# A fused attention, gate and expert kernel: a fifth tile for the rounded queries and keys, and transfers and loads asked for earlier

## The chip, the cores and the metric

The kernel runs on one core of one Trainium2 chip. The metric is the device time of one execution in microseconds, and of several executions the median is taken. PE is the TensorE matmul stream, DVE VectorE, ACT ScalarE, POOL GpSimd, and SP the engine whose queue issues nearly all the transfers here.

## What is computed

Three steps run one after the other on the same data: a causal attention with a decay, a gated layer, and a routing of each token to one of eight experts with a capacity.

```python
cum = np.cumsum(np.log(np.clip(f, 0.0001, 1.0)), axis=-1)          # 4 x 8 heads, 576 tokens, 64 wide
scores = q @ k.T / 8 + cum[:, None] - cum[None, :]                 # -1e9 above the diagonal
attn = softmax(scores)                                             # sum + 1e-9
x = (attn @ v).transpose(0, 2, 1, 3).reshape(2304, 512)
x = (sigmoid(x @ w_gate) * (x @ w_val)) @ w_out                    # 512 -> 1536 -> 512
logits = x @ w_route                                               # top scores first, at most 288 tokens each
out[tokens of e] = np.maximum(x[tokens of e] @ w1[e], 0) @ w2[e]   # 512 -> 1024 -> 512
```

## The kernel before

Attention takes the first 195 us, the gated layer the stretch to about 620 us, and routing and experts the rest. The change lies in attention and in the work that is fitted between its heads for the layer behind it.

**One head.** Queries and keys of a head (64 x 576 each) are used as a rounded part and a remainder. ACT writes the rounded parts into one of four tiles `P1` (`prep`, L116: two copies). Rows 64 and 65 of that tile take the decay of the head, two rows of `ck`, by a transfer (`decay`, L122). A second tile `P2` takes the rounded parts again, by two transfers (`copies`, L125), and the remainders, by two subtractions on POOL (`query_low` L134, `key_low` L137). `maxparts` (L148) then does four matmuls into two banks `a` and `c` of the ring `p1b`, and two more into `pb`, from `P1` alone; after each group DVE takes a row maximum over it (`top`, L156), five per head into five columns of `mx`. What a `top` writes beside the maximum goes to `junk`, a tile that nobody reads; the five have ranges of their own in it. `mrows` (L180) transposes `mx` with one matmul, ACT copies it to `mr`, and `mstore` (L186) sends it into row 66 of `P1`. With these rows `scores` (L189) gives, in twelve matmuls, exponents that are below zero already; ACT takes their exponentials, POOL blanks what lies above the diagonal (L211), and `av` (L216) multiplies with the values.

**The order.** It is written out by hand. In the steady part of the loop (L300) a turn does `scores(h)`, and then `av(h-1)` with two pieces put between its matmuls: `early` (row 66 of head h+2, `prep(h+4)` and `decay(h+4)`) and `late` (`maxpass(h+3)`). The four `P1` tiles go round by `h % 4`, so `decay(h+4)` can run when `scores(h)` is done with its tile, and its rows are read by `maxpass(h+4)` one turn later. The first heads (L261 to L347) are written out one by one, with empty matmuls (`warm`) between them to keep PE going.

**Work between the heads.** `fill(h)` (L1210) assembles the first fifteen of 36 pieces of the layer's weights: a transfer to `mr0` or `mr1`, three bit operations on DVE into `mb0` or `mb1` (L435 to L441), a rounding on ACT (L449), a subtraction on POOL (L452). From head 15 it also gets 512 tokens of attention's output ready in four parts of four turns: turn 0 issues four transfers (`XLoader.load`: the output, and the reciprocal sums spread over 64 partitions), turn 1 multiplies the two on DVE (L496), turn 2 rounds on ACT, turn 3 subtracts on POOL.

Of the kernel before, what the change touches and what calls it, by code (L numbers as in the profile page):

```python
# [58 lines left out]
KT = [(0, 0, 0, 1024), (0, 128, 128, 0), (0, 256, 256, 512), (0, 384, 384, 832), (0, 448, 512, 448)]  # L59


def attention(ev, qk, vr, f, xs, rec, fill):

# [1 line left out]
    with ExitStack() as ctx:  # L67
# [2 lines left out]
        ps2 = ctx.enter_context(tc.tile_pool(name="att_p2", bufs=1, space=PSUM))  # L70
        ps1 = ctx.enter_context(tc.tile_pool(name="att_p1", bufs=2, space=PSUM))

        ft = st.tile([NHEAD, S], F32, name="ft")
        nc.sync.dma_start(ft, f)

# [18 lines left out]
        nc.gpsimd.memset(zero, 0.0)  # L94
        nc.scalar.activation(idle, zero, AF.Ln, bias=1.0)
        next(consts)
        P1 = [st.tile([67, 64 + 2 * S], F32R, name=f"P1_{i}") for i in range(4)]
        for t in P1:
            nc.gpsimd.memset(t[64:67].bitcast(F32), 1.0)
            nc.gpsimd.memset(t[0:64, 0:64].bitcast(F32), 0.0)  # L100

        junk = st.tile([128, 1600], BF16, name="mj")
        JT = (0, 64, 256, 576, 1024)
        ck = st.tile([NHEAD, 2, S], F32R, name="ck")
        next(consts)
        nc.vector.tensor_scalar(ft, ft, 1e-4, 1.0, op0=OP.max, op1=OP.min)
# [7 lines left out]
        Q0, K0 = 64, 64 + S  # L114

        def prep(h):  # L116
            p1, r = P1[h % 4], RAW[h]
            nc.scalar.activation(p1[0:64, Q0:K0], r[0:64], AF.Copy)
            nc.scalar.activation(p1[0:64, K0:], r[64:128], AF.Copy)
            P2[h] = wk.tile([128, 2 * S], F32R, name="p2", bufs=4)  # L120

        def decay(h):  # L122
            nc.sync.dma_start(P1[h % 4][64:66, K0:].bitcast(F32), ck[h:h + 1].bitcast(F32))

        def copies(h, keys=True):  # L125
            p1, p2 = P1[h % 4], P2[h]
            nc.sync.dma_start(p2[0:64, :S].bitcast(F32), p1[0:64, Q0:K0].bitcast(F32))
            if keys:
                nc.sync.dma_start(p2[64:128, S:].bitcast(F32), p1[0:64, K0:].bitcast(F32))

        def key_copy(h):
            nc.vector.tensor_copy(P2[h][64:128, S:], P1[h % 4][0:64, K0:])

        def query_low(h):  # L134
            nc.gpsimd.tensor_tensor(P2[h][64:128, :S], RAW[h][0:64], P1[h % 4][0:64, Q0:K0], op=OP.subtract)

        def key_low(h):  # L137
            r, p2 = RAW.pop(h), P2[h]
# [9 lines left out]
        def maxparts(h):  # L148


            p1 = P1[h % 4]
            q = lambda s, e: p1[0:66, Q0 + s:Q0 + e]
            k = lambda s, e: p1[0:66, K0 + s:K0 + e]
            mx = MR[h] = wk.tile([128, 5], F32R, name="mx", bufs=3)

            def top(t, src):  # L156
                n = src.shape[-1]
                nc.vector.tensor_tensor_reduce(out=junk[:, JT[t]:JT[t] + n], in0=src, in1=ev.mq[:, S - n:], op0=OP.add,  # L158
                                               op1=OP.min, scale=-1.0, scalar=3e38, accum_out=mx[:, t:t + 1])

            a = ps1.tile([128, 512], F32, name="p1b")
            c = ps1.tile([128, 512], F32, name="p1b")
            mm(a[:, 0:192], q(64, 192), k(0, 192), True, False)
            mm(a[:, 192:512], q(192, 320), k(0, 320), False, True)
            mm(c[:, 0:448], q(320, 448), k(0, 448), True, False)
            mm(c[:, 448:512], q(-64, 64), k(0, 64), False, True)
            for t, src in ((1, a[:, 0:192]), (2, a[:, 192:512]), (3, c[:, 0:448]), (0, c[:, 448:512])):
                top(t, src)
            yield
            b = MT[h] = ps2.tile([128, 1024], F32, name="pb")  # L170
            mm(b[:, 256:512], q(448, 576), k(0, 256), True, True)
            mm(b[:, 512:832], q(448, 576), k(256, 576), True, True)
            top(4, b[:, 256:832])
            yield
# [9 lines left out]
            nc.scalar.activation(MR[h], b[0:5, 0:128], AF.Copy)  # L184

        def mstore(h):  # L186
            nc.sync.dma_start(P1[h % 4][66:67, 0:640].bitcast(F32), MR.pop(h))

        def scores(h, m=None):  # L189
            p1, p2 = P1[h % 4], P2.pop(h)  # L190
            y = ps2.tile([128, 1024], F32, name="py")
            x = ps1.tile([128, 512], F32, name="p1b")
            z = ps1.tile([128, 512], F32, name="p1b")

            def sc(out, k0, q0, q1, first=True, last=True):
                mm(out, p1[0:67, K0 + k0:K0 + k0 + 128], p1[0:67, Q0 + q0:Q0 + q1], first, False)
                mm(out, p2[:, S + k0:S + k0 + 128], p2[:, q0:q1], False, last)

            sc(y[:, 256:512], 0, 0, 256)
            sc(y[:, 512:832], 0, 256, 576)  # L200
            sc(x[:, 0:448], 128, 128, 576, last=False)
            sc(x[:, 448:512], 448, 512, 576, False)
            sc(z[:, 0:320], 256, 256, 576, last=False)
            sc(z[:, 320:512], 384, 384, 576, False)
            e = EX[h] = wk.tile([128, 1600], F32, name="e", bufs=3)
            for c0, c1, src in ((1024, 1600, y[:, 256:832]), (0, 512, x), (512, 1024, z)):
                nc.scalar.activation(e[:, c0:c1], src, AF.Exp, scale=0.125)

            for first, step, n, base in ((0, 512, 3, 0), (448, 384, 2, 64)):
                t = blocks(e, first, step, n)  # L210
                nc.gpsimd.affine_select(out=t, in_=t, pattern=[[-base, n], [1, 128]], compare_op=OP.is_ge, fill=0.0,  # L211
                                        base=base, channel_multiplier=-1)
            if m:
                mrows(m)
# [59 lines left out]
        copies(1, False)  # L274
        query_low(1)
        key_low(1)
        decay(2)
        decay(3)
        first = maxparts(1)
        next(first)  # L280
        mrows(0)
        mstore(0)
        load_v(0)
        next(first)
        prep(2)
        query_low(2)
        warm(WARM[2])
        mrows(1)
        mstore(1)
        load(3)  # L290
        scores(0)
        prep(3)
# [6 lines left out]
        key_low(3)  # L299
        for h in range(1, NHEAD):  # L300
            odd = h % 2
            if h == 2:
                mrows(3)
                mstore(3)
                load(4)
            scores(h)
            if h == 2:
                next(consts)
# [6 lines left out]
            def early():  # L315
                rows(h + 2)
                if h + 4 < NHEAD:
                    prep(h + 4)
                    decay(h + 4)

            def late():
                if h + 3 < NHEAD:
# [2 lines left out]
            if h == 1:  # L325

                def second():
                    rows(2)
                    decay(4)
                    decay(5)  # L330
                    load_v(1)
                    prep(4)

                av(0, {2: second, 3: lambda: maxpass(3)})
                copies(4)
                query_low(4)
            elif h == 2:
                prep(5)
                av(1)
                maxpass(4)  # L340
                key_low(4)
                query_low(5)
                copies(5)
            elif h == 3:

                def third():
                    prep(6)  # L347
                    decay(6)
                    decay(7)

                av(2, {2: lambda: rows(4), 3: lambda: maxpass(5), 5: third})
                prep(7)
                sixth = maxparts(6)
                next(sixth)
                rows(5)
                next(sixth)
                key_low(5)
                query_low(6)
                copies(6)
            else:  # L360
                av(h - 1, {AT[0]: early, AT[1]: late})
                if h < NHEAD - 3:
                    copies(h + 3)
# [38 lines left out]
class Weights:  # L402
# [4 lines left out]

    def __init__(self, ev, stage, w64):
        self.ev, self.stage, self.w64 = ev, stage, w64
        self.more, self.ahead = None, 2  # L410
        self.hi, self.lo, self.raw, self.b = [None] * NF, [None] * NF, {}, {}

    def tiles(self, pool, f0, f1):
# [3 lines left out]

    def load(self, n):
        f, i = divmod(n, 3)
        if f < NF:  # L420
            m = n % 4 if self.more else n % 2
            if m < 2:
                r = self.stage.tile([128, 512], I64, name=f"mr{m}", bufs=1)
            else:
                r = self.more.tile([128, 512], I64, name=f"bc{m - 2}", bufs=1)
            self.raw[n] = r
# [2 lines left out]
    def bits(self, n, step):  # L429
        if n < 3 * NF:  # L430
            nc = self.ev.nc
            w = self.raw[n].bitcast(U32).rearrange("p (n t) -> p n t", t=2)
            if step == 0:
                b = self.b[n] = self.stage.tile([128, 512], U32, name=f"mb{n % 2}", bufs=1)
                nc.vector.tensor_scalar(b, w[:, :, 1], 3, 0x3FFFFFF8, op0=OP.logical_shift_left, op1=OP.bitwise_and)  # L435
            elif step == 1:
                b = self.b[n]
# [736 lines left out]
EARLY = 15  # L1174
# [5 lines left out]
def network(tc, qk, vv, f, ww, bcT, w1, w2, cb, cf, out):  # L1180
# [3 lines left out]
    with ExitStack() as ctx:  # L1184
# [25 lines left out]
        def fill(h):  # L1210
# [3 lines left out]
            elif h == -2:  # L1214
                for step in range(3):
                    W.bits(0, step)
            elif h == -1:
                W.cut(0)
            count = lambda h: 3 + (h - 5) * (EARLY - 1) * 3 // 25
            jobs = lambda h: range(count(h), count(h + 1))  # L1220
# [5 lines left out]
            if XF <= h < XF + 16:  # L1226
                k, i = divmod(h - XF, 4)
                if i == 0:
                    X.load(0, k)
                else:  # L1230
                    X.split(0, k, steps=(i - 1,))

        attention(ev, qk, vv, f, xs, rec, fill)

        W.tiles(pool("w1", body), -(-EARLY // 3), NF)
        work, ps = ExitStack(), ExitStack()
# [84 lines left out]
```

## Time and profile before

| | |
|---|---|
| three executions | 902.11, 902.53, 905.34 us; median 902.53 |
| the profiled execution | 904.17 us, with a span of 902.1 us |
| PE busy | 879.2 us, 97% of the span |
| DVE, ACT, POOL busy | 60%, 38%, 51% |

The span is what the profile of the core covers; 2.07 us of the execution lie around it. A row of the timeline gives the start and the length of an instruction (of a few of the same form, with their count), and in brackets how long its engine had been idle before it and what released it. With PE at 97% the whole of its idle time is the first thing to look at, then the clock that it was granted, and then what the other engines do in the stretches in which PE waited.

### The profile page before, as it was taken

How to read it: one execution, taken by the hardware profiler on the slowest of the kernel's cores; microseconds unless marked ns; L12 is line 12 of the kernel's file. 1: busy time of each engine (PE TensorE's matmuls, PEld its weight loads, DVE VectorE, ACT ScalarE, POOL GpSimd, SP SyncE). 2: the span in 40 equal slices, each digit the busy share in tenths (PEclk: the TensorE clock that was granted, in tenths of full speed). 3: DMA queues.
4: the chain of work that ended last, by engine and by line, in shares of the span. 5: the costliest groups of instructions: out<-in, count | busy, mean ns of one | idle time of the engine just before them, and what ended most of it. 6: DMA issues, size and time to landing. Idle time of an engine off the chain costs nothing. (4 is left out here: it accounts for less than half of the span.)

```text
span 902.1 us, 14146 instructions
## 1 busy us (share of the span) xinstructions
PE 879.2 (97%) x5194; PEld 747.8 (83%) x5194; DVE 538.7 (60%) x1184; ACT 340.0 (38%) x602; POOL 461.1 (51%) x391
## 2 busy tenths in 40 slices
PE   8999999999999999999999999999999999999995
PEld 5688777778788888888888888887799999999995
DVE  6377877738886498989989642435523343434431
ACT  6677777642323211121121221221036454444530
POOL 7778889845565122221232221321159878777741
PEclk9899999999999999999999999999999999999998
DMA  5477888755551203010121210011247766656600
GB/s 164 131 221 228 231 234 242 202 142 174 170 175 65 76 1 93 18 56 21 41 71 27 68 47 1 1 45 48 72 144 246 233 205 182 187 187 206 204 29 27
DMA packets 48807, 110.87 MB, mean 123 GB/s; under 512 B 11328, under 2 KB 11744, under 8 KB 48736
## 3 DMA queue, kind: packets, MB, share of 16 engines
q1 hardware_dynamic: 44576, 98.41, 36.7%
q0 software_dynamic: 3072, 9.44, 3.3%
q10 hardware_dynamic: 1088, 2.10, 0.7%
q8 instruction: 41, 0.67, 0.3%
q14 instruction: 30, 0.25, 0.1%
HBM read 85.99 MB, written 14.57 MB: 111 GB/s over the span
## 5 line engine op out<-in xcount | busy, mean ns | idle before, releaser
L540 POOL TENSOR_TENSOR gl<-sg,gh 128x512 fp32r<-128x512 f32 x36 | 49.8, 1382 | 195.0 <-ACT gh L539 195.0
L1024 POOL TENSOR_TENSOR elo<-eraw,ehi 128x1024 fp32r<-128x1024 f32 x46 | 111.2, 2431 | 33.1 <-ACT ehi L1022 32.8
L531 PE MATMUL gv<-xah,w_hi 128*128 128x512 f32 (+1 forms) x288 | 102.3, 355 | 0.0
L531 PE MATMUL gv<-xal,w_hi 128*128 128x512 f32 (+1 forms) x288 | 101.9, 354 | 0.0
L531 PE MATMUL gv<-xah,w_lo 128*128 128x512 f32 (+1 forms) x288 | 101.8, 354 | 0.0
L142 PE MATMUL pv<-e,vf 128*65 128x256 f32 (+1 forms) x434 | 97.0, 361 | 0.7 <-DMA vf<-vv 0.4
L573 DVE CUSTOM_DVE_ANT_0 mb<-mb,bc 128x512 f32<-128x512 f32 x96 | 82.2, 856 | 3.3
L573 DVE CUSTOM_DVE_ANT_0 mb<-mr,bc 128x512 f32<-128x512 f32 x96 | 80.8, 842 | 2.8
L539 ACT ACTIVATE gh<-sg 128x512 fp32r<-128x512 f32 x36 | 22.8, 634 | 153.4 <-DVE sg L536 74.7
L1116 PE MATMUL ey<-hh,ehi 128*128 128x288 f32 x256 | 77.7, 304 | 0.0
L1116 PE MATMUL ey<-hl,ehi 128*128 128x288 f32 x256 | 75.8, 296 | 0.5
L531 PE MATMUL gv<-xbh,w_hi 128*128 128x512 f32 x192 | 75.9, 395 | 0.0
L1116 PE MATMUL ey<-hh,elo 128*128 128x288 f32 x256 | 75.3, 294 | 0.0
L531 PE MATMUL gv<-xbl,w_hi 128*128 128x512 f32 x192 | 74.9, 390 | 0.0
L531 PE MATMUL gv<-xbh,w_lo 128*128 128x512 f32 x192 | 74.8, 389 | 0.0
L142 PE MATMUL p1b<-P 66*128 66x192 f32 (+7 forms) x256 | 65.4, 324 | 5.0 <-DMA P<-ck 3.9
L158 DVE CUSTOM_DVE_ANT_0 mj<-p1b,mq 128x192 bf16<-128x192 f32 (+3 forms) x128 | 46.6, 419 | 37.9 <-PE p1b L142 37.5
L1103 PE MATMUL eh<-xeh,ehi 128*128 128x288 f32 x224 | 67.6, 302 | 0.0
L1022 ACT ACTIVATE ehi<-eraw 128x1024 fp32r<-128x1024 f32 x60 | 63.3, 1055 | 10.8 <-DMA eraw<-w 10.7
L1103 PE MATMUL eh<-xeh,elo 128*128 128x288 f32 x224 | 65.9, 294 | 0.0
L1103 PE MATMUL eh<-xel,ehi 128*128 128x288 f32 x224 | 65.8, 294 | 0.0
L1106 DVE SCALAR_TENSOR_TENSOR hl<-eh,hh 128x288 fp32r<-128x288 f32 x64 | 29.1, 456 | 61.5 <-ACT hh L1105 61.5
(215 smaller groups left out, 2274.4 us busy)
## 6 DMA issues: line engine op xcount, KB each, us to landing
eraw<-w SPq DMA_DIRECT2D x56, 512.0 KB
mr<-ww SPq DMA_DIRECT2D x26, 512.0 KB
raw<-qk SPq DMA_DIRECT2D x16, 576.0 KB
p<-P SPq DMA_DIRECT2D x62, 144.0 KB
vf<-vv SPq DMA_DIRECT2D x16, 330.0 KB
bc<-ww SPq DMA_DIRECT2D x10, 512.0 KB
xs<-xo SPq DMA_DIRECT2D x16, 292.5 KB
x2d<-mr SPq DMA_DIRECT2D x17, 256.0 KB
```

Source lines behind the costliest of these rows:

```text
L142: nc.tensor.matmul(out, lhsT, rhs, start=start, stop=stop, skip_group_check=True)
L158: nc.vector.tensor_tensor_reduce(out=junk[:, JT[t]:JT[t] + n], in0=src, in1=ev.mq[:, S - n:], op0=OP.add, op1=OP.min, scale=-1.0, scalar=3 ...
L531: nc.tensor.matmul(p[i][:, :m], w_[:, ws], x_[:, k], start=n == 0, stop=n == 11)
L539: nc.scalar.activation(hi, s, AF.Copy)
L540: nc.gpsimd.tensor_tensor(lo, s, hi, op=OP.subtract)
L573: nc.vector.tensor_tensor_reduce(out=junk, in0=a, in1=self.bc[j], op0=OP.mult, op1=OP.add, scale=1.0, scalar=0.0, accum_out=res)
L1022: nc.scalar.activation(hi, r, AF.Copy)
L1024: eng.tensor_tensor(lo, r, hi, op=OP.subtract)
L1103: nc.tensor.matmul(p[:, :CH], w_[:, ws], x_[:, k], start=n == 0, stop=n == 11)
L1106: nc.vector.scalar_tensor_tensor(h[1][:, f], p[:, :CH], 0.0, h[0][:, f], op0=OP.max, op1=OP.subtract)
L1116: nc.tensor.matmul(p[:, :CH], w_[:, ws], h_[:, f], start=n == 0, stop=n == 23)
```

## The change

The ring `P1` gets a fifth tile, and the ring index becomes `h % 5`. `early` sends `decay(h+5)` in place of `decay(h+4)`. The constant rows of the fourth and fifth tile are written by POOL after `key_low(1)` and no longer at the start. `junk` shrinks from 1600 columns to 576, and all `top`s write from its column 0. In the first heads, `mrows(3)`, `mstore(3)` and `load(4)` move behind `scores(2)`, and the decays and `prep(6)`, `prep(7)` move a head ahead. The weights get a third raw tile and a third assembled tile while attention runs, and their transfers are asked for three pieces ahead. The multiplication of attention's output moves from turn 1 to turn 2, and rounding and subtraction are both put into turn 3.

```diff
-        P1 = [st.tile([67, 64 + 2 * S], F32R, name=f"P1_{i}") for i in range(4)]
-        for t in P1:
+        P1 = [st.tile([67, 64 + 2 * S], F32R, name=f"P1_{i}") for i in range(5)]
+
+        def ones(t):
             nc.gpsimd.memset(t[64:67].bitcast(F32), 1.0)
             nc.gpsimd.memset(t[0:64, 0:64].bitcast(F32), 0.0)
 
-        junk = st.tile([128, 1600], BF16, name="mj")
-        JT = (0, 64, 256, 576, 1024)
+        for t in P1[:3]:
+            ones(t)
+
+        junk = st.tile([128, S], BF16, name="mj")
...
-                nc.vector.tensor_tensor_reduce(out=junk[:, JT[t]:JT[t] + n], in0=src, in1=ev.mq[:, S - n:], op0=OP.add,
+                nc.vector.tensor_tensor_reduce(out=junk[:, :n], in0=src, in1=ev.mq[:, S - n:], op0=OP.add,
...
         key_low(1)
+        for t in P1[3:]:
+            ones(t)
         decay(2)
-        decay(3)
         first = maxparts(1)
         next(first)
         mrows(0)
         mstore(0)
         load_v(0)
+        decay(3)
...
         mrows(1)
         mstore(1)
+        decay(4)
         load(3)
         scores(0)
...
-            if h == 2:
-                mrows(3)
-                mstore(3)
-                load(4)
             scores(h)
...
                     prep(h + 4)
-                    decay(h + 4)
+                if h + 5 < NHEAD:
+                    decay(h + 5)
...
                     rows(2)
-                    decay(4)
                     decay(5)
+                    decay(6)
...
             elif h == 2:
+                rows(3)
+                load(4)
                 prep(5)
                 av(1)
+                prep(6)
...
                 def third():
-                    prep(6)
-                    decay(6)
+                    prep(7)
                     decay(7)
+                    decay(8)
 
                 av(2, {2: lambda: rows(4), 3: lambda: maxpass(5), 5: third})
-                prep(7)
...
-        self.more, self.ahead = None, 2
+        self.third = None
+        self.more, self.ahead = None, 3
...
-            m = n % 4 if self.more else n % 2
+            m = n % 4 if self.more else n % (3 if n < EARLY else 2)
...
+            elif self.third:
+                r = self.third.tile([128, 512], I64, name="mr2", bufs=1)
...
-                b = self.b[n] = self.stage.tile([128, 512], U32, name=f"mb{n % 2}", bufs=1)
+                i = n % 3 if self.third else n % 2
+                b = self.b[n] = (self.third if i == 2 else self.stage).tile([128, 512], U32, name=f"mb{i}", bufs=1)
...
-                else:
-                    X.split(0, k, steps=(i - 1,))
+                elif i > 1:
+                    X.split(0, k, steps=(0,) if i == 2 else (1, 2))
```

Three places show what becomes of the order. In these rows the number behind a tile's name is the buffer, and a wait names the semaphore of the engine that sets it. The first is DVE at the first head's five `top`s. `mj` is `junk`, `p1b` and `pb` the score banks; each `top` is an instruction and a short one that reads its accumulator. Before:

```order
L158 ISA mj_130,mx_177<-p1b_178,mq_132 128x192 [waits PE_49]
L158 ISA mx_177 128x1
L158 ISA mj_130,mx_177<-p1b_178,mq_132 128x320
L158 ISA mx_177 128x1
L158 ISA mj_130,mx_177<-p1b_179,mq_132 128x448 [waits PE_49]
L158 ISA mx_177 128x1
L158 ISA mj_130,mx_177<-p1b_179,mq_132 128x64
L158 ISA mx_177 128x1
L158 ISA mj_130,mx_177<-pb_188,mq_132 128x576 [waits PE_49]
```

After:

```order
L162 ISA mj_129,mx_176<-p1b_177,mq_131 128x192 [waits PE_49]
L162 ISA mx_176 128x1
L162 ISA mj_129,mx_176<-p1b_177,mq_131 128x320 [waits DVE_49]
L162 ISA mx_176 128x1
L162 ISA mj_129,mx_176<-p1b_178,mq_131 128x448 [waits DVE_49,PE_49]
L162 ISA mx_176 128x1
L162 ISA mj_129,mx_176<-p1b_178,mq_131 128x64 [waits DVE_49]
L162 ISA mx_176 128x1
L162 ISA mj_129,mx_176<-pb_187,mq_131 128x576 [waits DVE_49,PE_49]
```

Each `top` now waits for DVE's own instruction before it. The second place is POOL at the start, from the third tile's constant rows on. Before:

```order
L99 MEMSET P1_2_120 3x1216
L100 MEMSET P1_2_120 64x64
L99 MEMSET P1_3_121 3x1216
L100 MEMSET P1_3_121 64x64
L135 TENSOR_TENSOR p2_167<-raw0_103,P1_0_118 64x576
L139 TENSOR_TENSOR p2_167<-raw0_103,p2_167 64x576
```

After:

```order
L101 MEMSET P1_2_120 3x1216
L102 MEMSET P1_2_120 64x64
L139 TENSOR_TENSOR p2_166<-raw0_103,P1_0_118 64x576
L143 TENSOR_TENSOR p2_166<-raw0_103,p2_166 64x576
L139 TENSOR_TENSOR p2_169<-raw0_103,P1_1_119 64x576
L143 TENSOR_TENSOR p2_169<-raw0_103,p2_169 64x576
L101 MEMSET P1_3_121 3x1216
```

The subtractions of heads 0 and 1 now come before the constant rows of the fourth tile. The third place is SP behind the first four transfers of attention's output, at about 158 us in the trace of before: row 66 (`mr`), the decay (`ck`), the two copies to `P2` and a load, and then the next turn. Before:

```order
L187 DMA P1_2_120<-mr_1831 1x5x128
L123 DMA P1_0_118<-ck_131 2x1x576
L127 DMA p2_1764<-P1_3_121 64x576
L129 DMA p2_1764<-P1_3_121 64x576
L81 DMA raw3_106<-qk 128x1152
L187 DMA P1_3_121<-mr_1893 1x5x128
L123 DMA P1_1_119<-ck_131 2x1x576
L127 DMA p2_1836<-P1_0_118 64x576
```

After:

```order
L191 DMA P1_1_119<-mr_1837 1x5x128
L127 DMA P1_4_122<-ck_130 2x1x576
L131 DMA p2_1770<-P1_2_120 64x576
L133 DMA p2_1770<-P1_2_120 64x576
L82 DMA raw3_106<-qk 128x1152
L191 DMA P1_2_120<-mr_1898 1x5x128
L127 DMA P1_0_118<-ck_130 2x1x576
L131 DMA p2_1842<-P1_3_121 64x576
```

Before, a decay goes to the tile whose copies follow one turn later (`P1_0`); now to one that is two turns away (`P1_4`).

## Rows read from the trace of the kernel before

**Rows 1.** The page: busy time of the engines, and granted clock in 40 slices.

```profile
PE 879.2 (97%) x5194; PEld 747.8 (83%) x5194; DVE 538.7 (60%) x1184; ACT 340.0 (38%) x602; POOL 461.1 (51%) x391
...
PEclk9899999999999999999999999999999999999998
```

**Rows 2.** Waits of PE: what for, us in total, times, longest us.

```profile
PE p1b L142 <- DMA P<-ck: 3.9, 4, 2.0
...
PE p1b L142 <- ACT P L119: 1.0, 1, 1.0
...
PE pv L142 <- DMA vf<-vv: 0.4, 1, 0.4
```

**Rows 3.** Windows: us, busy of PE, PEld, DVE, ACT, POOL, clock, DMA share, GB/s.

```profile
37.70:46.00 8.30, 8.30 (x36) 6.39 (x34) 2.04 (x9) 3.48 (x6) 3.15 (x5) 0.59 0.74 209
46.00:51.30 5.30, 5.30 (x35) 4.30 (x34) 4.00 (x14) 3.92 (x7) 3.09 (x4) 1.00 0.73 221
40.00:200.00 160.00, 155.34 (x929) 122.26 (x928) 110.56 (x305) 111.76 (x206) 128.53 (x125) 0.98 0.77 219
```

**Rows 4.** Timeline of POOL, start: constant rows, then subtractions.

```profile
5.55 1.10 POOL L99 MEMSET P<- 3x1216 f32 x1
...
7.14 1.87 POOL L135 TENSOR_TENSOR p<-raw,P 64x576 fp32r<-64x576 f32 x1
...
11.04 1.41 POOL L135 TENSOR_TENSOR p<-raw,P 64x576 fp32r<-64x576 f32 x1
...
22.50 2.78 POOL L139 TENSOR_TENSOR p<-raw,p 64x576 fp32r<-64x576 f32 x2 [2.28 <-DMA p<-P]
```

**Rows 5.** Timeline of DVE, start: decay, copies of keys, first `top`s.

```profile
6.18 0.78 DVE L110 TENSOR_SCALAR ck<-cum 32x576 fp32r<-32x576 f32 x1
...
7.78 1.92 DVE L132 CAST p<-P 64x576 fp32r<-64x576 f32 x2
...
10.65 0.08 DVE L158 DVE_READ_ACCUMULATOR2_ANT mx<- 128x1 fp32r x1
10.65 0.48 DVE L158 CUSTOM_DVE_ANT_0 mj<-p1b,mq 128x320 bf16<-128x320 f32 x1
```

**Rows 6.** Timeline of ACT: the first rounding, and one near 36 us.

```profile
5.23 0.68 ACT L118 ACTIVATE P<-raw 64x576 fp32r<-64x576 f32 x1 [0.46 <-DMA raw<-qk]
...
36.46 0.68 ACT L119 ACTIVATE P<-raw 64x576 fp32r<-64x576 f32 x1
```

**Rows 7.** Timeline of DVE at 308 us: routing's dot products, one scratch tile.

```profile
308.62 0.08 DVE L573 DVE_READ_ACCUMULATOR2_ANT L<- 128x1 f32 x1
308.74 0.69 DVE L573 CUSTOM_DVE_ANT_0 mb<-mr,bc 128x512 f32<-128x512 f32 x1
```

**Rows 8.** Timeline of PE: starts of row maxima, scores, and gaps.

```profile
9.84 0.73 PE L142 MATMUL p1b<-P 66*128 66x192 f32 x4 [0.70 <-DMA P<-ck]
...
14.64 0.41 PE L142 MATMUL pb<-identr,mx 128*5 128x128 f32 x1
...
35.63 0.72 PE L142 MATMUL p1b<-P 66*128 66x192 f32 x4 [0.59 <-DMA P<-ck]
...
37.35 0.53 PE L142 MATMUL pb<-P 66*128 66x256 f32 x2 [0.94 <-ACT mr L184]
...
63.22 0.39 PE L142 MATMUL p1b<-P 67*128 67x320 f32 x1
...
120.88 0.73 PE L142 MATMUL p1b<-P 66*128 66x192 f32 x4 [1.00 <-ACT P L119]
...
161.48 0.72 PE L142 MATMUL p1b<-P 66*128 66x192 f32 x4 [2.03 <-DMA P<-ck]
```

**Rows 9.** Timeline of SP's queue: the decay sent at 158 us.

```profile
157.98 0.68 SPq L123 DMA_DIRECT2D P<-ck  x1
```

**Rows 10.** Timeline of DVE: a fourth `top`; a first `top` without idle time.

```profile
61.99 0.22 DVE L158 CUSTOM_DVE_ANT_0 mj<-p1b,mq 128x64 bf16<-128x64 f32 x1
...
82.50 0.34 DVE L158 CUSTOM_DVE_ANT_0 mj<-p1b,mq 128x192 bf16<-128x192 f32 x1
```

More of the change, by code (lines that the diff above doesn't have):

```diff
@@ L59, with attention @@
 KT = [(0, 0, 0, 1024), (0, 128, 128, 0), (0, 256, 256, 512), (0, 384, 384, 832), (0, 448, 512, 448)]
-def attention(ev, qk, vr, f, xs, rec, fill):
+def attention(ev, qk, vr, f, xs, rec, fill, W):
     nc, tc = ev.nc, ev.tc
@@ L71, in attention @@
         ps1 = ctx.enter_context(tc.tile_pool(name="att_p1", bufs=2, space=PSUM))
+        W.third = st
         ft = st.tile([NHEAD, S], F32, name="ft")
@@ L116, in prep @@
         def prep(h):
-            p1, r = P1[h % 4], RAW[h]
+            p1, r = P1[h % 5], RAW[h]
             nc.scalar.activation(p1[0:64, Q0:K0], r[0:64], AF.Copy)
@@ L122, in decay @@
         def decay(h):
-            nc.sync.dma_start(P1[h % 4][64:66, K0:].bitcast(F32), ck[h:h + 1].bitcast(F32))
+            nc.sync.dma_start(P1[h % 5][64:66, K0:].bitcast(F32), ck[h:h + 1].bitcast(F32))
         def copies(h, keys=True):
-            p1, p2 = P1[h % 4], P2[h]
+            p1, p2 = P1[h % 5], P2[h]
             nc.sync.dma_start(p2[0:64, :S].bitcast(F32), p1[0:64, Q0:K0].bitcast(F32))
@@ L131, in key_copy @@
         def key_copy(h):
-            nc.vector.tensor_copy(P2[h][64:128, S:], P1[h % 4][0:64, K0:])
+            nc.vector.tensor_copy(P2[h][64:128, S:], P1[h % 5][0:64, K0:])
         def query_low(h):
-            nc.gpsimd.tensor_tensor(P2[h][64:128, :S], RAW[h][0:64], P1[h % 4][0:64, Q0:K0], op=OP.subtract)
+            nc.gpsimd.tensor_tensor(P2[h][64:128, :S], RAW[h][0:64], P1[h % 5][0:64, Q0:K0], op=OP.subtract)
         def key_low(h):
@@ L148, in maxparts @@
         def maxparts(h):
-            p1 = P1[h % 4]
+            p1 = P1[h % 5]
             q = lambda s, e: p1[0:66, Q0 + s:Q0 + e]
@@ L186, in mstore @@
         def mstore(h):
-            nc.sync.dma_start(P1[h % 4][66:67, 0:640].bitcast(F32), MR.pop(h))
+            nc.sync.dma_start(P1[h % 5][66:67, 0:640].bitcast(F32), MR.pop(h))
         def scores(h, m=None):
-            p1, p2 = P1[h % 4], P2.pop(h)
+            p1, p2 = P1[h % 5], P2.pop(h)
             y = ps2.tile([128, 1024], F32, name="py")
@@ L419, in load @@
         f, i = divmod(n, 3)
-        if f < NF:
-            m = n % 4 if self.more else n % 2
+        if f < NF and not (self.third and n > EARLY + 1):
+            m = n % 4 if self.more else n % (3 if n < EARLY else 2)
             if m < 2:
                 r = self.stage.tile([128, 512], I64, name=f"mr{m}", bufs=1)
+            elif self.third:
+                r = self.third.tile([128, 512], I64, name="mr2", bufs=1)
             else:
@@ L1217, in fill @@
             elif h == -1:
+                W.load(2)
                 W.cut(0)
@@ L1229, in fill @@
                     X.load(0, k)
-                else:
-                    X.split(0, k, steps=(i - 1,))
-        attention(ev, qk, vv, f, xs, rec, fill)
+                elif i > 1:
+                    X.split(0, k, steps=(0,) if i == 2 else (1, 2))
+        attention(ev, qk, vv, f, xs, rec, fill, W)
+        W.third = None
         W.tiles(pool("w1", body), -(-EARLY // 3), NF)
```

## The prediction

> **What bounds the kernel now.** I read the page's busy times first. PE is busy for 879.2 of 902.1 us [rows 1], so what the change can give in PE's own idle time is a part of the 22.9 us that remain, and no more. Then the granted clock: the second digit of forty and the last are below full speed [rows 1]. Then PE's waits: the largest kind by far is `P<-ck`, the decay's transfer, with 3.9 us in four waits, the longest 2.0 [rows 2]. The timeline of PE shows three of them: 0.70 before the first row maximum at 9.84, 0.59 at 35.63, and 2.03 at 161.48 [rows 8]; the fourth is what remains of 3.9, 0.6. A fifth wait of 1.00 at 120.88 carries the name of ACT's copy [rows 2, 8]; by SP's list the decay of that head landed just before it ended and the copy was long done, so I count it with them. The last view is windows: a head of the steady part takes 5.30 us at full clock (46.00 to 51.30), while the head from 37.70 to 46.00 took 8.30, PE busy all through, at a mean clock of 0.59 [rows 3]. That stretch follows the gap of 0.94 at 37.35 [rows 8].
>
> So the change works in attention alone, on some 4 us of waits for the decay and on the first 40 us. The rest of the program (46.00 on, but for those waits) has no edit on PE's side: the only PE instruction that changes place is the transposing matmul of `mrows(3)`.
>
> **The start, until scores(0).** Two parts of the change lengthen it.
>
> First, POOL. Its constant rows of the fourth tile (from 5.55) stood ahead of the first subtraction, which began at 7.14 [rows 4]. They are moved behind; the subtraction then waits only for ACT's copy, 5.23 plus 0.68, so it starts near 5.95 [rows 6]. At that time DVE is in the scan whose result the next instruction (6.18) turns into the decay [rows 5]. The two engines visibly hold each other up: the pair of casts at 7.78 takes 1.92 us and the first of them ends only after POOL's subtraction of 7.14 (7.14 + 1.87 = 9.01), while a subtraction that meets nothing takes 1.41 [rows 4, 5]. So I let the instruction at 6.18 end 0.36 after POOL's 5.95 + 1.41 = 7.36, at 7.72, where it now ends at 6.96: +0.76. The decay's second row, its transfer and PE's first row maximum (waiting for exactly that, 0.70 at 9.84 [rows 8]) go with it. Floor: 0, if the two do not meet.
>
> Second, the shared `junk`. Each `top` now waits for the one before. In the trace of before a `top` with its own range starts at 10.65, at the same time as the 0.08 us accumulator read ahead of it [rows 5]. The dot products of the routing do share a scratch tile: there the read at 308.62 ends at 308.70 and the next starts at 308.74 [rows 7]. The difference, from no later than the read's start to 0.04 after its end, is 0.12 us a `top`. Nine of the ten `top`s of heads 0 and 1 stand back to back ahead of `mrows(1)`: 9 x 0.117 = 1.05. Together 0.76 + 1.05 = 1.81: `mrows(1)` goes from 14.64 [rows 8] to 16.45, and scores(0) with it.
>
> **From there to 46 us.** `load(3)` now stands behind one more decay in SP's queue, and each turn of the copies is late by the same 1.8 and that issue (0.68, the length of such a row [rows 9]), in all 2.4 to 2.5. POOL's `key_low(2)` at 22.50 is released by such a copy [rows 4], and the scores of head 2, the masks behind and `av(1)` follow it; the chained `top`s add some 0.35 at the third head. Sum at 35 us: +2.9. Here something comes back: the 0.59 for the decay goes, since it is sent earlier, and of the 0.94 for ACT at 37.35 half goes, because ACT's copy of the row maxima stood behind the roundings of `prep(6)` (36.46 [rows 6]) that are now done a head earlier: 0.44. Net at scores(4): 2.9 - 0.59 - 0.44 = **+1.9**. Floor: -1.0 (both gaps go, no delay). Ceiling: +2.9.
>
> **The clock.** If PE keeps on through that place, the head behind it costs 5.30 and not 8.30 [rows 3]: **-3.0** from the profiled execution. It is the least sure term: PE's idle share there hardly changes by the sum above, but of the three timed executions two lie at 902.1 and 902.5 and one at 905.34, and the profiled one (904.17 with 2.07 around the span) is near the upper. The difference is what this stretch costs, so I read it as a thing that some executions have and others do not, and the median as one without it. The sum from the median then has no clock term.
>
> **The waits for the decay in the steady part.** 1.00 + 0.6 + 2.03 = 3.6 (120.88, the fourth, 161.48). At 161.48 the decay had been issued at 157.98, behind the first four transfers of attention's output and a raw weight [rows 9]; a head ahead is 5.3 us earlier [rows 3], more than any of these waits. What is late next: the values `vf`, for which PE waited 0.4 once already [rows 2] and whose transfers stand in the same queue; at 120.88 they would be about as late as the start that becomes possible. I take 0.4 back: **-3.2**. Floor of the gain -2.3 (that transfer becomes the wait at two of the three), ceiling -3.9 (all of 3.6 and a little of other waits).
>
> **The chained `top`s in the steady part.** Five per head, 4 to 5 of which gain a wait: 0.47 to 0.58 us per head on DVE. DVE is busy for 110.56 of 160 us from 40 to 200 [rows 3], so there is room on the mean. The tightest reader is the z bank of the scores: its matmul at 63.22 needs the bank that the fourth `top` (61.99 + 0.22, and its read: 62.3) empties [rows 8, 10], a slack of 0.9 to 1.0, of which some 0.35 goes. Covered, unless DVE comes to the `top`s late: at 82.50 the first `top` starts without idle time behind a weight piece [rows 10], and in seven of 26 heads it does. +0.3 (0 to +2). The one weight transfer more at the start of the loop: +0.2.
>
> **No cost or gain.** The third raw and third assembled tile take away DVE's waits for weights, and the multiplication one turn later its wait for transfers; DVE is not what PE waits for there, so 0, with the `top`s' room as the cover. If that cover is gone it is the third rival. Gated layer, routing and experts have the same instructions.
>
> **Sum.** From the profiled execution: 904.17 + 1.9 - 3.0 - 3.2 + 0.5 = 900.4. From the median: 902.53 + 1.9 - 3.2 + 0.5 = 901.7. I take the middle, **901.0**.
>
> **Rivals.** *The start is free* (17%): POOL and DVE do not meet, and the waits of the `top`s lie under PE's own work. Then 904.17 - 3.0 - 3.9 - 1.0 = 896.3 from the profile, 897.9 by a smaller gain at the decays. For it: the first subtraction has nothing to do with the decay in the program. Against: the casts of [rows 5].
>
> *The decays hide nothing* (10%): another transfer lands last at all three places, or the sent decay waits for its tile. Then the 3.2 shrink to about 1.5 and the time is 902 to 903. For it: the queue carries the same transfers in the same turn. Against: PE's waits name `vf` once, for 0.4 [rows 2].
>
> *DVE becomes the bound* (8%), the slower side: from the point at which the first `top` of a head starts more than 0.65 us late (1.0 of slack less 0.35), each further delay stops the z bank. At 0.25 us a head (half of the 0.5 that each head's chained `top`s add) over 26 heads that is 6.5: 901.0 + 6.5 = 907.5. For it: the heads without idle time (82.50). Against: 50 us of idle DVE [rows 3].
>
> *The chained waits are free* (5%): a `top` that waits for the one before starts as early as one that does not. The sum loses 1.05 + 0.35 + 0.3 = 1.7 and gives 899.3. For it: a start is only 0.04 behind the read at 308 us [rows 7]. Against: at 10.65 a start lies 0.08 ahead of the read's end [rows 5]. The Trainium skill, "VectorE: DVE Perf Modes", section "The DRAIN you can't avoid", says that eight copies with a semaphore after each take the same 13.88 us as with one after the last, so that "the semaphore costs nothing extra here"; by that rule the `top`s would cost nothing; the trace of before speaks against it for this kind of instruction, by the two starts just named.
>
> **How the numbers follow.** The forecast has 60%. A measurement of this kernel tells about 0.5% from no change, 4.5 us: faster is below 898.0, slower above 907.0. Faster: the first rival and a little of the forecast's lower end, 20%. Slower: the third and a little of the upper end, 9%. Same: 71%. The range takes the first rival's 896.5 in and ends at 905.0, where the start's ceiling (+1.0), the decays' floor (+0.9) and DVE's +2 meet; the third rival and half a tail stay out.
>
> **What would show it.** In the profile of after: no wait for `P<-ck` over 0.2 us past 40 us; the first row maximum near 10.6, `mrows(1)` near 16.4, and the read-to-start distance of `top`s near 0.04; scores(4) near 39.6; heads of 5.3 us. It is wrong if the first row maximum is at 9.8 (no meeting), if the clock falls again for some microseconds behind a gap, or if PE waits for DVE's `mx` or banks in the steady part.

## The result

The changed kernel takes 914.31 us in the median of four executions (912.04 to 915.40), the kernel before 902.50 (four, 902.11 to 905.34): a ratio of 1.0121, with a 95% interval from 1.0092 to 1.0149. It is slower by 12 us, where 901.0 was forecast with a range to 905.0. The profiled execution of after took 914.70, 10.53 more than that of before. Two later executions, one of e1_slot (971.60 us) and one of before (1234.98), ran at a far lower clock throughout than all others, and the medians and ratios below leave them out.

The page of after, its busy times and the granted clock, beside [rows 1]: PE is busy for 2.1 us more and idle for 8.5 us more, and the slice whose clock is clearly low is the ninth and no longer the second (near 195 us and not near 40).

```profile
PE 881.3 (97%) x5194; PEld 749.1 (82%) x5194; DVE 547.9 (60%) x1184; ACT 341.0 (37%) x602; POOL 462.4 (51%) x393
...
PEclk9999999989999999999999999999999999999998
```

PE's waits in after (what for, us in total, times, longest us), beside [rows 2]:

```profile
PE py L146 <- DMA P<-mr: 5.3, 2, 5.0
PE p1b L146 <- DVE mx L162: 2.7, 6, 1.6
...
PE pv L146 <- DMA vf<-vv: 2.4, 4, 0.9
PE p1b L146 <- DMA P<-ck: 1.8, 1, 1.8
...
PE py L146 <- DMA xs<-xo: 1.0, 1, 1.0
```

The decay (`P<-ck`) is waited for once, at the very start, and no longer at 35, 120, 143 and 161 us: this part did what it says. In its place stand one wait of 5.0 for a row of maxima (`P<-mr`), 2.7 us for DVE, 2.4 for the values (`vf`, 0.4 in before) and 1.0 for the store of attention's output (`xs<-xo`). The rows of PE at these places, and the first matmul of `scores(h)` for h = 4, 7, 29 and 31 around them, with h = 30 at 192.28:

```profile
40.10 0.28 PE L146 MATMUL py<-P 67*128 67x256 f32 x1
...
53.15 0.47 PE L146 MATMUL p1b<-P 67*128 67x448 f32 x1 [1.57 <-DVE mx L162]
...
59.80 0.53 PE L146 MATMUL py<-P 67*128 67x256 f32 x1
...
182.39 0.53 PE L146 MATMUL py<-P 67*128 67x256 f32 x1
...
192.28 0.55 PE L146 MATMUL py<-P 67*128 67x256 f32 x1 [5.03 <-DMA P<-mr]
...
199.00 0.53 PE L146 MATMUL py<-P 67*128 67x256 f32 x1
```

In before, the starts of `scores(h)` that [rows 3] does not have, for h = 7, 29, 30 and 31, are:

```profile
56.59 0.53 PE L142 MATMUL py<-P 67*128 67x256 f32 x1
...
179.04 0.53 PE L142 MATMUL py<-P 67*128 67x256 f32 x1
...
184.20 0.36 PE L142 MATMUL py<-P 67*128 67x256 f32 x1 [0.29 <-DMA P<-mr]
...
188.43 0.52 PE L142 MATMUL py<-P 67*128 67x256 f32 x1
```

From these starts and those between them comes a ledger. Each line is the time between two starts, or up to the first one:

| stretch | before | after | more |
|---|---|---|---|
| start to scores(4) | 37.72 | 40.10 | +2.38 |
| head 4 | 8.28 | 5.06 | -3.22 |
| head 5 | 5.30 | 5.62 | +0.32 |
| head 6 | 5.29 | 9.02 | +3.73 |
| heads 7 to 28 | 122.45 | 122.59 | +0.14 |
| head 29 | 5.16 | 9.89 | +4.73 |
| head 30 | 4.23 | 6.72 | +2.49 |
| sum, to scores(31) | 188.43 | 199.00 | +10.57 |

The sum is the whole difference of the two spans (10.6), so in these two executions nothing behind attention takes part. Windows of after (us, busy time of PE, PEld, DVE, ACT, POOL, clock, DMA share, GB/s) tell waiting from clock:

```profile
50.78:59.80 9.02, 7.23 (x34) 5.31 (x34) 5.57 (x18) 4.53 (x8) 5.11 (x6) 0.81 0.87 260
182.39:192.28 9.89, 4.86 (x29) 3.43 (x28) 5.35 (x13) 3.72 (x7) 3.78 (x4) 0.92 0.50 133
192.28:199.00 6.72, 6.72 (x27) 5.21 (x27) 0.65 (x1) 1.85 (x3) 3.57 (x4) 0.60 0.62 182
```

Head 6 waits for 1.8 us and spends 1.9 more because PE runs in part at 1.2 and not 2.4 GHz; head 29 waits for 5.0; head 30 waits for nothing, and its 2.5 are the lower clock alone. The low stretch that head 4 had before [rows 3] is gone, and two new ones are there.

**The wait of 5.03.** SP's queue around it (start and length of each issue):

```profile
177.97 0.39 SPq L87 DMA_DIRECT2D vf<-vv  x1
185.82 0.33 SPq L436 DMA_DIRECT2D mr<-ww  x1
...
189.05 0.76 SPq L191 DMA_DIRECT2D P<-mr  x1
```

and DVE's rows that it waits for:

```profile
178.75 1.62 DVE L445 TENSOR_SCALAR mb<-mr 128x512 uint32<-128x512 uint32 x1
180.40 0.69 DVE L448 SCALAR_TENSOR_TENSOR mb<-mr,mb 128x512 uint32<-128x512 uint32 x1
...
185.16 0.63 DVE L451 SCALAR_TENSOR_TENSOR mb<-mr,mb 128x512 uint32<-128x512 uint32 x1
```

For 7.5 us SP issues nothing. The transfer that stands first is that of weight piece 15. Pieces below 15 take raw tile n % 3; 15 takes 15 % 2, which is `mr1`, and there lies piece 13 (13 % 3 = 1), whose third bit operation (L451) ends at 185.79. In before piece 15 followed piece 13 as well, but its transfer was asked for two pieces ahead, when piece 13 was done; three ahead it is asked for while piece 13 is still being assembled. Row 66 of head 30, issued at 189.05, had nothing to do with weights and stood behind it.

### The profile page after: what moved, and what is told of

The parts are those of the page before. It is cut to its first block, busy times and chain, and to the rows that moved or that the text cites. A ratio compares the mean times of both kernels' runs of the same rounds, so it can differ in the third digit from the quotient of the medians.

```text
span 912.7 us, 14162 instructions
## 1 busy us (share of the span) xinstructions
PE 881.3 (97%) x5194; PEld 749.1 (82%) x5194; DVE 547.9 (60%) x1184; ACT 341.0 (37%) x602; POOL 462.4 (51%) x393
## 5 line engine op out<-in xcount | busy, mean ns | idle before, releaser
L162 DVE CUSTOM_DVE_ANT_0 mj<-p1b,mq 128x192 bf16<-128x192 f32 (+3 forms) x128 | 54.3, 424 | 38.9 <-PE p1b L146 31.6
L146 PEld LDWEIGHTS pv<-e,vf 128*65 128x65 f32 x434 | 50.3, 140 | 19.4 <-issue 7.9
```

The costliest lines, as they stand in the source:

```text
L146: nc.tensor.matmul(out, lhsT, rhs, start=start, stop=stop, skip_group_check=True)
L162: nc.vector.tensor_tensor_reduce(out=junk[:, :n], in0=src, in1=ev.mq[:, S - n:], op0=OP.add, op1=OP.min, scale=-1.0, scalar=3e38, accum_ou ...
```

## The experiments

Theories after the result: A, the tile of piece 15 blocks SP's queue; B, the chained `top`s cost what separate ranges would give back; C, POOL's subtraction holds up the decay at the start; F, head 6 is lost since DVE comes late to the first weight piece; and the plain rival that the decays gained nothing. The experiments ran in three groups, each beside before: e1 to e4 (median of before 902.32), e5 to e8 (903.47) and e9 to e11 (902.32). "Of before" is the ratio within a group; medians of different groups are less comparable.

**Piece 15 into a free tile** (e1_slot).

```diff
-            m = n % 4 if self.more else n % (3 if n < EARLY else 2)
+            m = n % 4 if self.more else ((1 - n) % 3 if n < EARLY else n % 2)
```

> The kernel after with one edit: the raw tiles of the first fifteen weight pieces go round by (1 - n) % 3 and not by n % 3, so that piece 15, which takes the tile mr1 by n % 2, finds there piece 12 and no longer piece 13. Theory A (the transfer of piece 15 stands first in SP's queue and waits until DVE has done with piece 13; the row maxima of head 30 are queued behind it): PE's wait of 5.03 us at 192.28 shrinks to 0.3, the head behind it runs at full clock again (4.2 and not 6.7 us), in all 7.2 us less: about 907.1. Rival (SP's queue is late there because of the traffic of the third tiles, whatever the tile): the wait stays above 3 us and the time within 2 us of 914.3.

905.05 us (nine executions), 1.0035 of before (1.0008 to 1.0061). The place in SP's queue and at PE, and the head behind:

```profile
177.90 1.42 SPq L436 DMA_DIRECT2D mr<-ww  x1
...
181.88 0.76 SPq L191 DMA_DIRECT2D P<-mr  x1
```

```profile
187.74 0.35 PE L146 MATMUL py<-P 67*128 67x256 f32 x1 [1.07 <-DMA P<-mr]
```

```profile
187.74:191.97 4.23, 4.23 (x27) 3.33 (x27) 0.48 (x1) 1.82 (x4) 2.89 (x4) 1.00 0.86 260
```

The queue's hole of 7.5 us is gone, heads 29 and 30 take 10.16 in place of 16.61, and PE runs the last head at full clock. The wait left is 1.07 and not 0.3. A holds: 9.3 us between the medians and 6.8 between the profiled executions, of which these two heads show 6.5.

**Separate ranges in `junk`** (e2_junk). The five share 1024 columns in a way that neighbours do not overlap:

```diff
-        junk = st.tile([128, S], BF16, name="mj")
+        junk = st.tile([128, 1024], BF16, name="mj")
+        JT = (960, 0, 192, 512, 0)
...
-                nc.vector.tensor_tensor_reduce(out=junk[:, :n], in0=src, in1=ev.mq[:, S - n:], op0=OP.add,
+                nc.vector.tensor_tensor_reduce(out=junk[:, JT[t]:JT[t] + n], in0=src, in1=ev.mq[:, S - n:], op0=OP.add,
```

> The kernel after with one edit: junk has 1024 columns, and the row maxima of one head that follow each other write to separate ranges (only the fifth shares one with the first two). Theory B (each chained row maximum costs 0.12 to 0.2 us on DVE, 0.72 a head): the five of a head take 2.15 us and not 2.85; scores(0) comes 1.0 to 1.4 us earlier than 17.05; PE's waits for row maxima (1.57 at 53.15 among them) lose 0.7 each; the time is 911.5 to 913. If the stretch at lower clock behind 53.15 goes with the wait, 909.5. Rival (a wait for one's own engine costs nothing): all starts stay, 914.3 within 0.7.

910.30 (four executions; 1.0110, 1.0075 to 1.0145). Rows of one head's `top`s, in after and then in this kernel:

```profile
44.32 0.08 DVE L162 DVE_READ_ACCUMULATOR2_ANT mx<- 128x1 fp32r x1
44.44 0.49 DVE L162 CUSTOM_DVE_ANT_0 mj<-p1b,mq 128x320 bf16<-128x320 f32 x1
44.86 0.08 DVE L162 DVE_READ_ACCUMULATOR2_ANT mx<- 128x1 fp32r x1
45.09 0.62 DVE L162 CUSTOM_DVE_ANT_0 mj<-p1b,mq 128x448 bf16<-128x448 f32 x1
```

```profile
41.65 0.08 DVE L163 DVE_READ_ACCUMULATOR2_ANT mx<- 128x1 fp32r x1
41.65 0.49 DVE L163 CUSTOM_DVE_ANT_0 mj<-p1b,mq 128x320 bf16<-128x320 f32 x1
```

With its own range a `top` starts with the accumulator read ahead of it; with a shared one 0.12 later (44.32 to 44.44), and 0.23 later where it waits for PE's bank too (44.86 to 45.09). B holds for the `top`s and the start: scores(0) starts at 15.82 and not 17.05. The wait at head 6 is 0.96 in place of 1.78, and that head takes 6.55 in place of 9.02; this is less surely the edit's doing, since e6_x, which has separate ranges too, waits 2.62 there. The wait for piece 15 stays (4.96). The median lies 4.0 us below after's, but the two intervals overlap.

**The fourth tile's constant rows at the start** (e3_pool).

```diff
-        for t in P1[:3]:
+        for t in P1[:4]:
             ones(t)
...
-        for t in P1[3:]:
+        for t in P1[4:]:
```

> The kernel after with one edit: the constant rows of the fourth tile are written at the start again, ahead of POOL's first subtraction; only the fifth tile's come later. Theory C (POOL's subtraction now meets DVE's computation of the decay and holds it up): the first row maximum comes 0.7 us earlier than 10.54, scores(0) too, and the time is 913.0 to 914.3. Rival (the first row maximum is late for another reason): it stays at 10.5.

915.25 (four executions; 1.0148, 1.0101 to 1.0194). The time does not tell this kernel from after; the traces do. POOL and DVE in after:

```profile
5.84 1.52 POOL L139 TENSOR_TENSOR p<-raw,P 64x576 fp32r<-64x576 f32 x1 [0.33 <-ACT P L122]
```

```profile
6.19 1.49 DVE L114 TENSOR_SCALAR ck<-cum 32x576 fp32r<-32x576 f32 x1
```

and PE's first row maximum in this kernel, at 10.54 in after:

```profile
9.83 0.33 PE L146 MATMUL p1b<-P 66*128 66x192 f32 x1 [1.44 <-DMA P<-ck]
```

The 0.71 comes back (C), as does as much at scores(0), 16.34. A wait of 2.1 us at head 6 takes 0.5 of what was gained, and scores(31) still starts 0.4 earlier than in after (198.61). That this execution nevertheless takes 1.1 us more (915.77 against 914.70) arises behind attention.

**The three together** (e4_three).

> The kernel after with the three edits together (piece 15 to a free tile, separate ranges in junk, the fourth tile's constant rows at the start). If the three are what the change cost, and the decays' waits are gained: the start of scores(5) stands near 43, no gap over 1 us behind it, and the time is 899 to 902. If the low clock that went from 38 us comes back at another place in the first 60 us: 902 to 905. Rival (something else costs more): over 906.

900.08 (ten executions), 0.9982 of before (0.9953 to 1.0010): within what was expected. scores(5) starts at 42.01, heads 7 to 28 take 119.84 and not 122.45, and the wait at head 6 is 0.92. These three edits together account for the change's loss: 14 us between the medians of after and of this kernel.

**The decays alone, on the kernel before** (e5_decay). The fifth tile and each decay a head earlier, and nothing else of the change:

```diff
...
-                    decay(h + 4)
+                if h + 5 < NHEAD:
+                    decay(h + 5)
...
```

> The kernel before with one part of the change alone: the fifth P1 tile, with each decay sent a head earlier (its constant rows written after key_low(1)); junk, the weights' tiles, the order of the first heads and the multiplication stay as before. Theory D (the decays' waits go, and the values' transfers, late next, take a part back): no wait for P<-ck past 35 us; heads 18, 22 and 25 at 5.3 us in place of 6.5, 6.1 and 7.6; 0.5 to 1.5 us of new waits for vf; the end of attention 2.5 to 3 us earlier; time 899.3 to 900.3. Rival (the values and row maxima take all of it back): within 0.7 us of before.

900.54 (ten executions), 0.9972 of before (0.9952 to 0.9992). PE's waits in it:

```profile
PE pb L145 <- ACT mr L187: 2.1, 2, 1.7
PE pv L145 <- POOL p L142: 1.2, 1, 1.2
...
PE p1b L145 <- DVE mx L161: 0.8, 1, 0.8
PE p1b L145 <- DMA P<-ck: 0.3, 1, 0.3
```

D holds for the decays: heads 7 to 28 take 119.82 in place of 122.45, 2.6 less, the rest taken back by a wait of 1.2 at 133.59 and one of 0.8 at 159.85. These are for POOL and DVE; the new waits for `vf` that D expected did not come. What I did not expect is the first row: with the decay early, the wait for ACT's copy of the maxima at 37 us grows from 0.94 [rows 8] to 1.75, because it is the same end that is waited for.

**The multiplication in its old turn** (e6_x: the three edits, and turns 1, 2, 3 again):

```diff
-                elif i > 1:
-                    X.split(0, k, steps=(0,) if i == 2 else (1, 2))
+                else:
+                    X.split(0, k, steps=(i - 1,))
```

> The kernel with the three edits (e4_three), and the multiplication, rounding and subtraction of attention's output in turns 1, 2 and 3 as before. Theory E (rounding and subtraction both in turn 3 stand ahead of the exponentials and POOL's key remainders, and PE waits 1.0 us at 165 us for it): that wait goes, head 27 takes 5.3 and not 6.5 us, the time is 1.0 less than e4_three: 899.1. Rival (the multiplication a turn earlier waits on DVE for its transfers and makes the row maxima late): a wait of PE for DVE's mx of 0.5 us or more in one of heads 16, 20, 24, 28, and no gain.

900.99 (ten executions; 0.9971, 0.9940 to 1.0001), which the times do not tell from e4_three's 900.08 (0.9982). The expected wait at head 27 does go (6.46 to 5.28 us for that head), and the rival's comes, at head 26 and not at one of the four named: DVE waits for the multiplication's transfers and PE for the `top`s behind.

```profile
159.07 0.69 DVE L507 TENSOR_TENSOR xr<-xal,xr 128x512 f32<-128x512 f32 x1 [1.97 <-DMA xr<-rec]
```

```profile
160.50 0.47 PE L147 MATMUL p1b<-P 67*128 67x448 f32 x1 [1.06 <-DVE mx L163]
```

So theory E fell in its sum: heads 26 and 27 together take 11.94 us here and 11.61 in e4_three, so the later turn is worth about as much as it costs.

**The first weights a head earlier** (e7_weights, on the three edits):

```diff
-FIRST = {3: -3, 4: -2, 5: -1}
+FIRST = {2: -3, 4: -2, 5: -1}
```

> The kernel with the three edits (e4_three), with the first two weight transfers asked for one head earlier. Theory F (at 49 us PE waits 0.92 us for row maxima because DVE comes to the first weight piece late, its transfer landing behind the point that PE has reached): DVE's first bit operation starts 4 us or more earlier, the wait goes, head 6 takes 5.3 and not 6.5 us; 1.2 us less than e4_three: 898.9. Rival (the transfers then hold up those of the heads 4 and 5): the wait goes but others of PE (for P or the copies' remainders) of about the same size come before 49 us; 900.1.

898.46 (ten executions), 0.9948 of before (0.9928 to 0.9969). DVE's first bit operation starts at 43.39, 2.2 us earlier than in e4_three (45.62) where 4 or more was expected, the wait goes all the same, and head 6 takes 5.27 in place of 6.52:

```profile
47.64:52.91 5.27, 5.27 (x35) 4.27 (x34) 3.33 (x12) 4.25 (x8) 4.96 (x6) 1.00 0.73 174
```

F holds here.

**Both** (e8_all).

> The kernel with the three edits and the two of e6_x and e7_weights together. If both theories hold: 897.9, 0.5% below the kernel before, with the end of attention 8 us earlier than before; if both rivals hold: 900 to 901.

897.22 (twelve executions), 0.9935 of before (0.9915 to 0.9955), the lowest median, though nothing parts it from e7_weights (the means are 898.55 and 898.39). That the median lies near the 897.9 of "both hold" is luck: E had fallen in e6_x. The profiled execution, at 901.80, is one of the long ones: it has the wait for `top`s at head 26 (2.26 us), and that head takes 10.68, PE busy for 8.41 of it:

```profile
156.18:166.86 10.68, 8.41 (x33) 6.27 (x34) 5.96 (x18) 5.11 (x9) 6.36 (x7) 0.68 0.69 200
```

**The first weights a head earlier, in after** (e9_early: the same edit, the three others left out).

> The kernel after with one edit: the first two weight transfers are asked for one head earlier, as in e7_weights; the transfer of piece 15, the shared junk and the constant rows stay as in after. Theory F (head 6 of after takes 9.0 us, 3.7 more than a head of 5.3, because DVE comes late to the first weight piece, and the stretch at lower clock behind follows from that wait): the wait of 1.57 at 53.15 goes and head 6 takes 5.3 to 5.6; the 5.0 at 192 stays; time 910 to 911.5. Rival (the chained row maxima alone make the wait): a wait over 1 us stays at head 6, time 913 to 915.

913.14 (four executions, 907.48 to 915.55; 1.0115, 1.0049 to 1.0181): by the times, nothing is shown, and the median lies where the rival put it. In the trace, of the execution with 907.48, head 6 is whole:

```profile
50.27:55.56 5.29, 5.29 (x35) 4.28 (x34) 2.97 (x12) 4.25 (x8) 4.98 (x6) 1.00 0.73 174
```

The wait of 4.86 for piece 15 stays, with 6.48 for head 30. All the traces together bear F out. What counts is how far DVE's first bit operation starts ahead of scores(6). It is 3.3 to 4.3 us in before, e5_decay and the five kernels that ask for the weights a head earlier (e7_weights, e8_all, e9_early, e10_two, e11_order), and head 6 takes 5.27 to 5.29 in all seven. It is 2.1 us or less in the other six (after 1.5, e4_three 1.9, e6_x 0.8 behind), and there head 6 takes 6.5 to 9.5. That the late weights cost head 6 its time is thus shown by traces; their share in the median is not.

**Two weight tiles as before** (e10_two: e7_weights without the third tiles, two pieces ahead, and so without the fault at piece 15).

> The kernel e7_weights with the weights' tiles as in the kernel before: two raw and two assembled tiles in attention, transfers two pieces ahead. Theory G (the third tiles take away waits of DVE that PE does not feel): within 1 us of e7_weights, 898 to 899.5, DVE again waits some microseconds for weights. Rival (with the other waits gone DVE's lateness is felt): waits of PE for mx of 1 us or more in all, time over 900.5.

898.37 (ten executions; 0.9951, 0.9918 to 0.9983), e7_weights' time to 0.1. DVE's waits from 40 to 190 us:

```profile
DVE mb L446 <- POOL w_lo L463: 6.9, 3, 3.1
DVE mb L446 <- ACT P L123: 3.0, 1, 3.0
DVE mb L446 <- DMA mr<-ww: 1.3, 1, 1.3
```

e7_weights has none of these. So the third tiles take away 11.2 us of DVE's waiting and nothing of PE's waits for DVE, 0.3 us in either trace (G).

**The first heads' order as before** (e11_order: e7_weights with `mrows(3)` ahead of scores(2), and `prep(6)`, `prep(7)` at head 3).

> The kernel e7_weights with the order of the first heads as in the kernel before: mrows(3), mstore(3) and load(4) ahead of scores(2), prep(6) and prep(7) at head 3. Theory H (the new order is worth what the wait for ACT's copy of the row maxima at 37 us loses): that wait is 0.9 to 1.8 and not 0.41, scores(4) comes 0.3 to 1.3 later than 37.2, and in some executions a stretch at lower clock of up to 3 us follows; time 899 to 901.5. Rival (the order changes nothing once the decays are early): scores(4) within 0.2 us of 37.2, time within 0.7 of 898.5.

900.40 (ten executions; 0.9958, 0.9924 to 0.9991). ACT and PE at the place:

```profile
37.19 0.68 ACT L124 ACTIVATE P<-raw 64x576 fp32r<-64x576 f32 x1
37.78 0.25 ACT L189 ACTIVATE mr<-pb 5x128 f32<-5x128 f32 x1
```

```profile
38.08 0.43 PE L147 MATMUL pb<-P 66*128 66x256 f32 x1 [1.75 <-ACT mr L189]
```

```profile
38.58:46.70 8.12, 8.12 (x34) 6.24 (x34) 1.88 (x7) 3.48 (x6) 2.58 (x5) 0.60 0.46 116
```

The wait is 1.75 where the new order has 0.41, and a head at a mean clock of 0.60 follows: scores(5) at 46.70 and not 42.36. In the medians, 1.9 us more than e7_weights and 2.0 more than e10_two of the same group. H holds in the trace; the medians of ten point the same way and their intervals overlap.

## Why the prediction was wrong

**The failed step is "No cost or gain".** It let the third tiles go at 0 because DVE is not what PE waits for. That is right for the tiles (e10_two) and misses the transfers that fill them: each is an instruction in SP's queue, and the change alters which tile it waits for. The rule `n % (3 if n < EARLY else 2)` stood in the diff; following piece 15 by hand to `mr1` and piece 13 would have shown the wait, and the row behind it in the queue is a row of maxima that PE waited for even before, by 0.3 us (184.20 in the rows of before). It is 7.2 of 10.6 us in the profiled executions (heads 29 and 30), 4.7 as waiting and 2.5 as clock. From the profiled execution the sum forecast -3.8 us and +10.6 came. Of these 14.4 us, 7.2 are this step, 4.1 heads 5 and 6, 2.8 the steady part (heads 7 to 28) and 0.3 the start with head 4.

**The rival that DVE becomes the bound was right in its mechanism and wrong in its place.** I priced it as 0.25 us at each of 26 heads; it came, in the main, at one. (By the trace of before its heads without idle time are eight of 25, two of them behind the multiplication, and not seven of 26 behind a weight piece.) DVE waits 2.37 us for the first weight piece, whose transfer lands at 49.27, and one of the three operations on it takes 1.83, beside a subtraction on POOL from 49.60 to 51.01, where the like one at 51.59 takes 0.69:

```profile
49.27 0.43 DVE L445 TENSOR_SCALAR mb<-mr 128x512 uint32<-128x512 uint32 x1 [2.37 <-DMA mr<-ww]
49.73 1.83 DVE L448 SCALAR_TENSOR_TENSOR mb<-mr,mb 128x512 uint32<-128x512 uint32 x1
51.59 0.69 DVE L451 SCALAR_TENSOR_TENSOR mb<-mr,mb 128x512 uint32<-128x512 uint32 x1
52.20 0.35 DVE L162 CUSTOM_DVE_ANT_0 mj<-p1b,mq 128x192 bf16<-128x192 f32 x1
```

The `top`s of head 8 start at 52.20, 3.4 after the first matmul that they read (48.76). Two of the sum's own terms bring this about. The delay at the start pushes the weight's transfer back (issued at 42.81 and not 40.45), and the head at low clock that is gone at 38 us lets PE come to the place 0.5 us earlier than before. DVE had been given that time by PE's slowness. Of DVE's lead of 3.4 us in before 1.5 are left: 1.3 went with the later landing, 0.5 with PE's earlier coming. So 3.0 us of gain was booked, rightly (-3.22), and 3.73 were lost two heads later, for which the sum had no term.

**The start** was right in its parts: the first row maximum at 10.54 (forecast 10.60), the meeting of POOL and DVE, 1.49 us for the instruction that took 0.78 [rows 5] and an end at 7.68 (forecast 7.72). The Trainium skill, "SBUF — State Buffer", section "SBUF: two separate sides", calls the port pair that the two share an exclusive lock, held for a whole instruction, when VectorE's instruction runs in a two-port mode or has two SBUF inputs. The trace agrees in the order of the two ends: POOL, which started first (5.84), ends at 7.36, and DVE, started at 6.19, at 7.68. `mrows(1)` came at 16.99 and not 16.45, scores(4) at +2.38 and not +1.9. What was too small at the start is the price of a chained `top`: 0.12 where it waits for DVE alone, and 0.23 where PE's bank is waited for as well, so 0.7 us a head and not 0.5. The rival that these waits are free falls with the rows of e2_junk. The Trainium skill's sentence quoted ahead, of "VectorE: DVE Perf Modes", section "The DRAIN you can't avoid", was measured on copies; for this kind of instruction the trace does not agree.

**The decays** were right as a mechanism, the floor of -2.3 to the ceiling of -3.9 holding the 2.6 of e5_decay. In after nothing of it is seen (+0.14 for heads 7 to 28). The term that failed is what I let other waits take back, 0.4: PE waits there 2.4 us for the values, 1.0 for the store of attention's output, 0.6 for ACT and 0.4 for the `top`s. With `top`s apart the same heads take 119.5 to 119.8 us in e2_junk, e4_three, e7_weights and e10_two. But e9_early, with chained `top`s, takes 120.1, and e1_slot 120.6, so the shared range does not alone explain after's 122.6; what decides when the values come late is open.

**The 0.94 at 37.35:** the half that was to come back did, but it was more than half of 0.94: without the new order the wait would have grown to 1.75 (e5_decay, e11_order). I had priced the new order at 0.44; with the decays early its absence costs 1.34 (a wait of 1.75 in place of 0.41) and, in the two traces just named, a stretch at lower clock behind it.

## What to carry to other kernels

Where a ring of buffers changes its length at some index, follow the first index on each side by hand to the tile that it takes and to the one who last read it; a transfer that waits for a tile holds up everything behind it in its queue, and the price is that of the row with the least slack there. Scratch output that nobody reads is a dependence all the same: separate ranges for neighbours undo it. And when a wait or a slow stretch of the bounding engine goes, ask which other engine had used that time to keep up.

## What the runs showed of the hardware

In these traces the lower clock follows waits of PE, but the length of the wait does not decide it. A wait of 1.75 us near 38 us was followed by 8.12 us for a head in e11_order and by 6.69 in e5_decay, against about 5.1 at full clock (e7_weights). One of 2.26 at 159 us (e8_all) cost 3.1 more, one of 1.57 (after, head 6) 1.9 more; one of 2.62 at 51.59 in e6_x cost nothing beyond itself:

```profile
48.17:56.24 8.07, 5.45 (x33) 4.27 (x34) 6.10 (x19) 4.53 (x8) 4.84 (x5) 1.00 0.68 183
```

The executions of one kernel lie several us apart: those of e10_two are five from 895.9 to 896.6 and five from 900.1 to 901.9. The mean granted clock of the first five is 0.996 to 0.998, that of the others 0.993 to 0.996. So the longer ones do run at a lower clock; as only one execution of each kernel has a trace, where in them it falls is open.
